# TensorE in a written order from the 24th head on, with shorter transposes, in a window attention and feed-forward kernel

## The chip, the cores and the metric

The kernel runs on one core of a Trainium2 chip. Its engines are TensorE (PE: matmuls; PEld: the loads of the stationary operand), VectorE (DVE), ScalarE (ACT), GpSimd (POOL) and SyncE (SP, which issues most DMAs here). The metric is the device time of one execution, in microseconds; lower is better. Three runs of the kernel before were timed.

## The reference

Two layers follow each other. Attention over 8 batches and 8 heads (512 local and 32 global positions, head size 64), in which a local query sees the 32 global keys and local keys at a distance of at most 32, and a global query sees everything; then a feed-forward layer over all 4352 rows.

```python
# attention, per batch and head; D = 64, window = 32, scale = 1/8
k_all, v_all = concat(k_g, k_l), concat(v_g, v_l)
out_g = softmax(scale * q_g @ k_all.T) @ v_all
s_ll = where(abs(i - j) <= 32, scale * q_l @ k_l.T, -1e9)
s_l = concat(scale * q_l @ k_g.T, s_ll)
out_l = softmax(s_l) @ v_all
x = rows of concat(out_g, out_l), heads side by side        # 4352 x 512
# feed-forward, d_model 512, d_ff 2048; s and b are scalars
r = relu(x @ w_in)
out = (s * r * r + b) @ w_out
```

## The kernel before

**Slots.** A *slot* j is one head of one half of the 512 local positions: 8 batches x 2 halves x 8 heads = 128 slots, 16 per batch. The 256 queries of a slot are two blocks of 128; each block has its keys in two chunks. `CHUNKS` gives for each chunk its first key column `c0`, the first query row `q0` that it serves and the number `n` of such rows: one chunk serves all 128 rows, the other one only 64 or 96 of them.

**Precision.** From slot `NF` = 16 on, and in the feed-forward layer throughout, operands are split into a high part (fp32r) and a low one, and products are sums of several matmuls over these parts. The first 16 slots use plain f32 matmuls (`scores32`, `transposes32`, `pv32`).

**A split slot.** `scores(j)`: four matmuls into `ps_s` (L362), and one into `ps_g` (L368) for the global queries; then `softmax(j)` on DVE, ACT and DVE (L213, L219, L226). `p_transposes(j)`: four TensorE transposes of the probabilities `sm` into `ps_t` (L310), split by ACT and DVE (L378, L379). `pv_products(j)`: four matmuls into `ps_o` (L389), summed in `pv_sum` (L400 to L403) into the tile `x`. `transposes_and_pv(j-1, j-2)` mixes the transposes of the slot before with the products of the one before that, two and two.

**Global queries.** Per batch and group g of four heads: `g_softmax` at slot 16b + G_AT[g], `g_transposes` three slots later (four chunks "early", the fifth "late" in the slot, L441; evacuated by L444 and L445), `g_load` (a DMA and splits on ACT and POOL) and `g_pv` (ten matmuls, L463) in the slots after. The results go to DRAM (`xg_d`). The transposes of heads and of global groups use one and the same PSUM buffer, tag "t".

**Feed-forward.** 17 token tiles of 256 rows (16 of the two halves of the batches, the last one of the global rows), 8 steps each: step m does `ffn_in(m)` (24 matmuls of 256 columns, L511; then ACT L517, DVE L518, ACT L525 and DVE L526 make `g`) and `ffn_out(m)` (12 matmuls of 512 columns, L543). `x_split(t)` (L483, L484) makes a tile's operand `xs`, which has a single buffer. The last tile's operand comes from `xg_split`, which loads two row blocks from `xg_d` into buffers of tag "r" (two buffers, used by the feed-forward steps too), transposes each (L494) and splits it (L496, L497).

**Weights.** w_in and w_out arrive as 64-bit integers in 32 pieces and are decoded on ACT and DVE in slots 0 to 13 (`PIECES`).

**What sets the order.** The text is a loop over j; in pass j stand the scores of slot j, the transposes of j - 1, the products of j - 2, ffn_in of m = j - LAG and ffn_out of m - 1. The framework's planner turns this into one instruction stream per engine: at each moment of its own timeline it takes, of the instructions that are ready, the one that stands first in the text. So the text gives priorities and the planner's costs the order. `tc.manual_schedule(engines=...)` fixes an engine's order to that of the text; the kernel before doesn't use it. Each engine then executes its stream strictly in that order and waits for what each instruction needs.

Of the kernel before, what the change touches and what calls it, by code (L numbers as in the profile page):

```python
# [10 lines left out]
F32 = mybir.dt.float32  # L11
# [10 lines left out]
P = 128  # L22
# [21 lines left out]

NF = 16
AHEAD = 0
LAG = 12
WARM_FIRST = 28
WARM_HEAD = 0

# [2 lines left out]
NORM_POOL = lambda j: j < NF  # L53
ACT_DMA = 2
X_ACT = lambda j: j >= 8
G_AT = (13, 18)
G_TR = 3
G_LD = (0, 2)
G_PV = (1, 3)
# [9 lines left out]
def window_attention_then_ffn(ctx: ExitStack, tc: tile.TileContext, qd, qg, kw, vw, vg, w_in, w_out, sv, bv, out):  # L69
    nc = tc.nc  # L70
# [4 lines left out]
    ps = ctx.enter_context(tc.tile_pool(name="ps", bufs=1, space=bass.MemoryType.PSUM))  # L75
# [3 lines left out]
    ident = const.tile([P, P], F32, name="ident")  # L79
# [9 lines left out]
    def keep_busy(n, name):  # L89
        p_w = ps.tile([P, 512], F32, tag="acc1", name=name)  # L90
        for _ in range(n):
            nc.tensor.matmul(p_w, lhsT=warm[:, 0:P], rhs=warm, start=True, stop=True)
# [5 lines left out]
    for first, parts in ((True, ((32, 192, 0),)), (False, ((0, 160, 0), (192, 224, 32)))):  # L98
# [3 lines left out]
        for c0, c1, skip in parts:  # L102
            for sign, base in ((1, c0 - skip), (-1, 64 - c0 + skip)):
                nc.gpsimd.affine_select(
                    out=mask[:, c0:c1], in_=mask[:, c0:c1], pattern=[[sign, c1 - c0]], compare_op=ALU.is_ge,
# [56 lines left out]
    st_ = {}  # L162

    def slot(j):
        return j // 16, (j // 8) % 2, j % 8
# [38 lines left out]
    def softmax(j, p_s):  # L204
        b, hf, h = slot(j)
        sm = sb.tile([P, NC], F32, tag="sm", name=f"sm{j}")
        nm = sb.tile([P, 2], F32, tag="nm", name=f"nm{j}")
        ss = sb.tile([P, 2], F32, tag="ss", name=f"ss{j}")
        cols = [COLS[hf, blk] for blk in range(2)]
        for blk in range(2):  # L210
            c = cols[blk]
            mask = masks[hf == 0 and blk == 0][:, 0:c.stop - c.start]
            nc.vector.tensor_tensor_reduce(  # L213
                out=sm[:, c], in0=p_s[:, c], in1=mask,
                op0=ALU.add, op1=ALU.min, scale=-scale, scalar=BIG, accum_out=nm[:, blk:blk + 1],
            )
        for blk in range(2):
            p = sm[:, cols[blk]]
            nc.scalar.activation(  # L219
                out=p, in_=p, func=AF.Exp, bias=nm[:, blk:blk + 1], scale=-1.0, accum_out=ss[:, blk:blk + 1],  # L220
            )
        nc.vector.tensor_scalar_add(ss, ss, 1e-9)
        nc.vector.reciprocal(ss, ss)
        for blk in range(2):
            p = sm[:, cols[blk]]
            (nc.gpsimd if NORM_POOL(j) else nc.vector).tensor_scalar(  # L226
                out=p, in0=p, scalar1=ss[:, blk:blk + 1], scalar2=1.0, op0=ALU.mult, op1=ALU.mult,
            )
        st_["p", j] = sm


    def own(k, hf):
        n, c = (192, P) if hf == 0 else (240, 144)
        return k[:, 0:2 * n].rearrange("p (k c) -> p k c", k=2)[:, :, 0:c]

    def sg_rows(j):
        b, hf, h = slot(j)
        if hf == 0 and h % 4 == 0:
            st_["sg", b, h // 4] = sb.tile([P, SGW], F32, tag=f"sg{h // 4}", name=f"sg{j}", bufs=1)
        r0 = 32 * (h % 4)  # L240
        return st_["sg", b, h // 4][r0:r0 + 32]
# [30 lines left out]
    def scores32(j):  # L272
        b, hf, h = slot(j)
        if WARM_HEAD and j < LAG:
            keep_busy(WARM_HEAD, f"warm{j + 1}")
# [15 lines left out]
    def chunks(j):  # L291
        b, hf, h = slot(j)
        o = 0
        for blk in range(2):
            for c in range(2):
                c0, q0, n = CHUNKS[hf, blk][c]
                yield blk, c, c0, q0, n, slice(o, o + n)
                o += n
# [4 lines left out]
    def p_transposes(j):  # L303
        sm = st_.pop(("p", j))
        p_t = ps.tile([P, 512], F32, tag="t", name=f"ps_t{j}")
        first = 64 if slot(j)[1] == 0 else 0
        st_["pst", j] = p_t[:, first:first + NC]
        for blk, c, c0, q0, n, o in chunks(j):
            at = first + o.start - q0
            nc.tensor.transpose(out=p_t[:, at:at + P], in_=sm[:, c0:c0 + P], identity=ident)  # L310
            if c == 1:
                yield

    def transposes32(j):
        list(p_transposes(j))
# [39 lines left out]
    def scores(j):  # L355
        b, hf, h = slot(j)
        ks, qs = st_.pop(("ks", j)), st_.pop(("qs", j))
        p_s = ps.tile([P, 512], F32, tag="s", name=f"ps_s{j}")
        for blk in range(2):
            cols = COLS[hf, blk]  # L360
            for a in range(2):
                nc.tensor.matmul(  # L362
                    p_s[:, cols], lhsT=qs[:, a, blk * P:(blk + 1) * P], rhs=ks[:, cols], start=(a == 0), stop=(a == 1),
                )
        p_g = ps.tile([P, 512], F32, tag="g", name=f"ps_g{j}")
        qgh = st_["qgs", b][:, h]
        ng = 256 + 32 * hf
        nc.tensor.matmul(p_g[0:64, 0:ng], lhsT=qgh, rhs=own(ks, hf), start=True, stop=True)  # L368
        softmax(j, p_s)

        tg = sb.tile([P, 288], F32, tag="tg", name=f"tg{j}", bufs=1)
        nc.scalar.copy(out=tg[0:32, 0:ng], in_=p_g[32:64, 0:ng])
        nc.vector.tensor_add(out=sg_rows(j)[:, hf * 256:hf * 256 + ng], in0=p_g[0:32, 0:ng], in1=tg[0:32, 0:ng])
# [11 lines left out]
    def pv_products(j):  # L385
        pt, vs = st_.pop(("pt", j)), st_.pop(("vs", j))
        p_o = st_["pso", j] = ps.tile([P, 2, 2, P], F32, tag="o", name=f"ps_o{j}")
        for blk, c, c0, q0, n, o in sorted(chunks(j), key=lambda x: (x[0], -x[1])):
            nc.tensor.matmul(  # L389
                p_o[:, blk, :, q0:q0 + n], lhsT=vs[:, 2 * blk + c], rhs=pt[:, :, o], start=(c == 1), stop=(c == 0),  # L390
            )
            if c == 0:
                yield

    def pv_sum(j):
        b, hf, h = slot(j)
        p_o = st_.pop(("pso", j))
        x = x_tile(j)
        u = sb.tile([P, 2, P], F32, tag="u", name=f"u{j}", bufs=1)
        nc.scalar.copy(out=u, in_=p_o[:, :, 1, :])  # L400
        nc.vector.tensor_add(out=u, in0=p_o[:, :, 0, :], in1=u)
        q0 = 64 * (h % 2)
        nc.vector.tensor_add(  # L403
            out=x[q0:q0 + 64, h // 2, :].rearrange("p (k q) -> p k q", k=2), in0=u[0:64], in1=u[64:128],
        )


    def transposes_and_pv(jt, jp):
        t = p_transposes(jt) if NF <= jt < NS else iter(())
        p = pv_products(jp) if NF <= jp < NS else iter(())  # L410
        for _ in range(2):
            next(p, None)
            next(t, None)
        list(p), list(t)
        if NF <= jp < NS:
            pv_sum(jp)
        if NF <= jt < NS:
            p_split(jt)
# [145 lines left out]
    extra, early, late = defaultdict(list), {}, {}  # L564
    for b in range(B):
        for g in range(2):
            s0 = 16 * b + G_AT[g]
            extra[s0].append(lambda b=b, g=g: g_softmax(b, g))
            early[s0 + G_TR] = lambda b=b, g=g: g_transposes(b, g, 0, 4)
            late[s0 + G_TR] = lambda b=b, g=g: g_transposes(b, g, 4, 5)  # L570
            for i in range(2):
                h = 4 * g + 2 * i
# [13 lines left out]
    sp = pick(lambda j: None, split)  # L586
    vl, vl32 = pick(lambda j: None, v_load), pick(v_load32, lambda j: None)
    sc = pick(scores32, scores)
    tr = pick(transposes32, lambda j: None)
    vsp = pick(lambda j: None, v_split)  # L590
    pvs = pick(pv32, lambda j: None)
    piece = 0
    qg_load(0)
    ld(0)
    ld(1)
    for j in range(NM + LAG + 2):
        sp(j + 1)
        ld(j + 2)
        vl(j)
        for _ in range(PIECES[j] if j < len(PIECES) else 0):  # L600
            weight_piece(piece)
            piece += 1
        if j < NS:
            b1 = j // 16 + 1
            if j == 14 and NF > 16:
                qg_load32(1)
            elif j % 16 == 14 and b1 < B:
                qg_load(b1)
            sc(j)
            if j == NF - 1 and NF % 16:  # L610
                if NF > 16:
                    qg_load(j // 16)
                qg_split(j // 16)
            if j % 16 == 15 and NF <= j + 1 < NS:
                qg_split(b1)
        if j in early:
            early.pop(j)()
        m = j - LAG
        if m == 0:
            x_split(0)  # L620
        if 0 <= m < NM:
            ffn_in(m)
            if m % 8 == 7:
                t = m // 8 + 1
                if t < 16:
                    x_split(t)
                elif t == 16:
                    xg_split(16)
        tr(j - 1)
        transposes_and_pv(j - 1, j - 2)  # L630
        vsp(j - 1)
        for fn in extra.pop(j, []):
            fn()
        pvs(j - 2)
        vl32(j)
        if 0 <= m - 1 < NM:
            ffn_out(m - 1)
        if j in late:
            late.pop(j)()
    assert piece == 32 and not extra  # L640


# [66 lines left out]
```

## Time and profile before

| | |
|---|---|
| time, median of 3 runs | 1067.21 us (1065.12 to 1070.13) |
| the profiled execution's own time | 1068.86 us |
| its span, first to last instruction | 1067.1 us |
| TensorE busy | 1039.9 us (97%) |
| VectorE / ScalarE / GpSimd busy | 813.6 / 706.9 / 330.7 us |
| mean granted TensorE clock | 0.966 |
| bytes moved | 86.79 MB |

The page also follows back the chain of work that ended last. 93% of it is on PE: ffn_in 36%, ffn_out 35%, the transposes of heads 6%, scores 4%, products 4%. The busy time of PE has modelled ends, so the spacing of its instructions is read from the chain, in which a group's time runs to the start of the next.

### The profile page before, as it was taken

How to read it: one execution, taken by the hardware profiler on the slowest of the kernel's cores; microseconds unless marked ns; L12 is line 12 of the kernel's file. 1: busy time of each engine (PE TensorE's matmuls, PEld its weight loads, DVE VectorE, ACT ScalarE, POOL GpSimd, SP SyncE). 2: the span in 40 equal slices, each digit the busy share in tenths (PEclk: the TensorE clock that was granted, in tenths of full speed). 3: DMA queues.
4: the chain of work that ended last, by engine and by line, in shares of the span. 5: the costliest groups of instructions: out<-in, count | busy, mean ns of one | idle time of the engine just before them, and what ended most of it. 6: DMA issues, size and time to landing. Idle time of an engine off the chain costs nothing.

```text
span 1067.1 us, 20496 instructions
## 1 busy us (share of the span) xinstructions
PE 1039.9 (97%) x7076; PEld 932.2 (87%) x7076; DVE 813.6 (76%) x2116; ACT 706.9 (66%) x1796; POOL 330.7 (31%) x397
## 2 busy tenths in 40 slices
PE   6989999999999999999999999999999999999996
PEld 2558899999999999999999999999999999999895
DVE  6789777997788887888788877888788878853221
ACT  5667676786677776786678766867677767743221
POOL 3222433442343342342344233434234224211000
PEclk7558999999999999999999999999999999999999
DMA  7656321321323131221122122312122122100000
GB/s 248 199 180 209 96 86 52 93 92 34 97 68 98 53 97 52 90 79 60 58 92 84 56 80 69 95 56 84 60 79 89 53 72 77 59 14 34 22 20 20
DMA packets 63535, 86.79 MB, mean 81 GB/s; under 512 B 7624, under 2 KB 50632, under 8 KB 63432
## 3 DMA queue, kind: packets, MB, share of 16 engines
q1 hardware_dynamic: 63144, 84.44, 25.1%
q8 instruction: 56, 0.92, 0.3%
q10 hardware_dynamic: 288, 1.05, 0.3%
q14 instruction: 47, 0.39, 0.1%
HBM read 76.02 MB, written 9.44 MB: 80 GB/s over the span
## 4 chain that ended last, share of the span: by engine, by line
PE 93%; DMA 2%; ACT 2%; DVE 2%; POOL 1%; issue 0%; SPq 0%; ACTq 0%; DVEq 0%; POOLq 0%
PE ps_h L511 36%; PE acc L543 35%; PE ps_t L310 6%; PE ps_s L362 4%; PE ps_o L389 4%; PE ps_og L463 2%; PE ps_o L327 2%; PE ps_s L281 1%; PE ps_g L368 1%; DMA wst<-in_w_in 1%; PE ps_g L287 1%; PE ps_tg L441 1%; DMA rk<-in_kw 1%; POOL sm L226 0%; DMA wst<-in_w_out 0%
## 5 line engine op out<-in xcount | busy, mean ns | idle before, releaser
L511 PE MATMUL ps_h<-xs,wi 128*128 128x256 f32 x3264 | 449.8, 286 | 0.9 <-ACT xs L496 0.7
L511 PEld LDWEIGHTS ps_h<-xs,wi 128*128 128x128 f32 x3264 | 418.0, 190 | 11.1 <-ACT xs L483 0.9
L543 PE MATMUL acc<-wo,g 128*128 128x512 f32 x1632 | 417.3, 395 | 0.0
L543 PEld LDWEIGHTS acc<-wo,g 128*128 128x128 f32 x1632 | 292.2, 188 | 54.0 <-ACT x L333 0.5
L518 DVE SCALAR_TENSOR_TENSOR r<-ps_h,s_t,r 128x512 f32<-128x512 f32 x136 | 101.5, 746 | 79.1 <-ACT r L517 78.9
L201 POOL TENSOR_TENSOR vs<-rv,vs 128x256 fp32r<-128x256 f32 x112 | 85.3, 761 | 190.7 <-ACT vs L200 190.3
L526 DVE SCALAR_TENSOR_TENSOR g<-r,b_t,g 128x512 fp32r<-128x512 f32 x136 | 109.3, 804 | 45.1 <-ACT g L525 41.7
L525 ACT ACTIVATE g<-r,b_t 128x512 fp32r<-128x512 f32 x136 | 98.4, 724 | 65.0 <-DVE r L518 64.8
L517 ACT ACTIVATE r<-ps_h 128x512 f32<-128x512 f32 x136 | 81.2, 597 | 87.5 <-PE ps_h L511 79.7
L193 POOL TENSOR_TENSOR kq<-rq,kq 128x256 fp32r<-128x256 f32 x112 | 89.3, 797 | 149.1 <-ACT kq L192 130.4
L219 ACT ACTIVATE sm<-sm,nm 128x224 f32<-128x224 f32 (+1 forms) x256 | 118.3, 465 | 24.4 <-DVE nm L213 23.6
L310 PE MATMUL ps_t<-ident,sm 128*128 128x128 f32 x512 | 100.6, 288 | 4.2 <-POOL sm L226 4.2
L191 POOL TENSOR_TENSOR kq<-rk,kq 64x416 fp32r<-64x416 f32 x56 | 63.1, 1127 | 121.0 <-ACT kq L190 105.4
L213 DVE CUSTOM_DVE_ANT_0 sm<-ps_s,mask 128x224 f32<-128x224 f32 (+1 forms) x256 | 85.8, 367 | 16.1 <-PE ps_t L310 9.5
L455 POOL TENSOR_TENSOR vsg<-rvg,vsg 128x320 fp32r<-128x320 f32 x64 | 58.0, 927 | 98.2 <-ACT vsg L454 98.2
L389 PE MATMUL ps_o<-pt,vs 128*128 128x256 f32 x448 | 83.7, 283 | 0.1
L403 DVE TENSOR_TENSOR x<-u 64x256 f32<-64x256 f32 x112 | 71.0, 634 | 3.6
L362 PE MATMUL ps_s<-kq 128*128 128x192 f32 (+1 forms) x448 | 72.9, 275 | 0.0
L310 PEld LDWEIGHTS ps_t<-ident,sm 128*128 128x128 f32 x512 | 58.2, 145 | 14.8 <-POOL sm L226 7.4
L362 PEld LDWEIGHTS ps_s<-kq 128*128 128x128 f32 x448 | 65.3, 190 | 5.1
L226 DVE TENSOR_SCALAR sm<-sm,ss 128x192 f32<-128x192 f32 (+1 forms) x224 | 66.9, 341 | 3.2
L389 PEld LDWEIGHTS ps_o<-pt,vs 128*128 128x128 f32 x448 | 66.8, 190 | 2.1 <-DVE pt L379 0.6
(79 smaller groups left out, 1232.4 us busy)
## 6 DMA issues: line engine op xcount, KB each, us to landing
rq<-in_qd SPq DMA_DIRECT2D x128, 128.0 KB, 2.1
rv<-in_vw SPq DMA_DIRECT2D x128, 128.0 KB, 2.0
rk<-in_kw SPq DMA_DIRECT2D x64, 208.0 KB, 2.4
rvg<-in_vg SPq DMA_DIRECT2D x32, 320.0 KB, 2.9
out<-o SPq DMA_DIRECT2D x34, 256.0 KB, 2.1
wst<-in_w_in SPq DMA_DIRECT2D x15, 512.0 KB, 4.5
wst<-in_w_out SPq DMA_DIRECT2D x15, 512.0 KB, 4.5
rqg<-in_qg SPq DMA_DIRECT2D x8, 128.0 KB, 2.0
```

The costliest lines, as they stand in the source:

```text
L193: nc.gpsimd.tensor_sub(out=qs[:, 1, :], in0=rq, in1=f32(qs[:, 0, :]))
L201: nc.gpsimd.tensor_sub(out=vs[:, :, 1, :], in0=rv4, in1=f32(vs[:, :, 0, :]))
L213: nc.vector.tensor_tensor_reduce(out=sm[:, c], in0=p_s[:, c], in1=mask, op0=ALU.add, op1=ALU.min, scale=-scale, scalar=BIG, accum_out=nm[: ...
L219: nc.scalar.activation(out=p, in_=p, func=AF.Exp, bias=nm[:, blk:blk + 1], scale=-1.0, accum_out=ss[:, blk:blk + 1],)
L310: nc.tensor.transpose(out=p_t[:, at:at + P], in_=sm[:, c0:c0 + P], identity=ident)
L362: nc.tensor.matmul(p_s[:, cols], lhsT=qs[:, a, blk * P:(blk + 1) * P], rhs=ks[:, cols], start=(a == 0), stop=(a == 1),)
L389: nc.tensor.matmul(p_o[:, blk, :, q0:q0 + n], lhsT=vs[:, 2 * blk + c], rhs=pt[:, :, o], start=(c == 1), stop=(c == 0),)
L511: nc.tensor.matmul(p_h[:, k], lhsT=wi[:, a, c, f * P:(f + 1) * P], rhs=xs[:, e, c, :], start=(n == 0), stop=(n == 11),)
L518: nc.vector.scalar_tensor_tensor(out=r, in0=p_h, scalar=s_t, in1=r, op0=ALU.mult, op1=ALU.mult)
L525: nc.scalar.activation(out=g[:, 0], in_=r, func=AF.Identity, bias=b_t)
L526: nc.vector.scalar_tensor_tensor(out=g[:, 1], in0=r, scalar=b_t, in1=f32(g[:, 0]), op0=ALU.add, op1=ALU.subtract,)
L543: nc.tensor.matmul(oacc[t][i], lhsT=g[:, a, k, i * P:(i + 1) * P], rhs=wo[:, e, f, :], start=(pr == 0 and n == 0), stop=(pr == 7 and n == 5),)
```

## The change

- `LAG` is 10 in place of 12: each feed-forward step stands two slots earlier in the text, and the loop has two passes less.
- From pass j = `ORDERED` = 24 on, PE's instructions are issued in the order of the text. The other engines are left to the planner.
- In a pass, transposes and products now stand ahead of ffn_in (with the v splits and v loads that follow them), and the early global transposes behind it.
- `G_AT` is (12, 16) in place of (13, 18).
- A chunk that serves 64 or 96 rows from row 0 is transposed with 96 rows in place of 128; the short chunks of both blocks come first.
- Transposes and products alternate two products, three transposes, two products, one transpose.
- The matmul into `ps_g` stands between two of the four matmuls of the scores.

```diff
-LAG = 12
+LAG = 10
+ORDERED = 24
-G_AT = (13, 18)
+G_AT = (12, 16)
 ...
         first = 64 if slot(j)[1] == 0 else 0
         st_["pst", j] = p_t[:, first:first + NC]
-        for blk, c, c0, q0, n, o in chunks(j):
+        for blk, c, c0, q0, n, o in sorted(chunks(j), key=lambda x: x[1]):
             at = first + o.start - q0
-            nc.tensor.transpose(out=p_t[:, at:at + P], in_=sm[:, c0:c0 + P], identity=ident)
-            if c == 1:
-                yield
+            q = 96 if c == 0 and q0 == 0 else P
+            nc.tensor.transpose(out=p_t[:, at:at + q], in_=sm[0:q, c0:c0 + P], identity=ident[0:q, 0:q])
+            yield
 ...
             for a in range(2):
                 nc.tensor.matmul(
                     p_s[:, cols], lhsT=qs[:, a, blk * P:(blk + 1) * P], rhs=ks[:, cols], start=(a == 0), stop=(a == 1),
                 )
-        nc.tensor.matmul(p_g[0:64, 0:ng], lhsT=qgh, rhs=own(ks, hf), start=True, stop=True)
+                if blk == hf and a == 0:
+                    nc.tensor.matmul(p_g[0:64, 0:ng], lhsT=qgh, rhs=own(ks, hf), start=True, stop=True)
 ...
                 p_o[:, blk, :, q0:q0 + n], lhsT=vs[:, 2 * blk + c], rhs=pt[:, :, o], start=(c == 1), stop=(c == 0),
             )
-            if c == 0:
-                yield
+            yield
 ...
-        for _ in range(2):
-            next(p, None)
-            next(t, None)
+        for which in (p, p, t, t, t, p, p, t):
+            next(which, None)
         list(p), list(t)
 ...
+    fixed = ExitStack()
     for j in range(NM + LAG + 2):
+        if j == ORDERED:
+            fixed.enter_context(tc.manual_schedule(engines={mybir.EngineType.PE}))
         sp(j + 1)
 ...
-        if j in early:
-            early.pop(j)()
+        tr(j - 1)
+        transposes_and_pv(j - 1, j - 2)
+        vsp(j - 1)
+        pvs(j - 2)
+        vl32(j)
         m = j - LAG
         if m == 0:
             x_split(0)
 ...
-        tr(j - 1)
-        transposes_and_pv(j - 1, j - 2)
-        vsp(j - 1)
+        if j in early:
+            early.pop(j)()
         for fn in extra.pop(j, []):
             fn()
-        pvs(j - 2)
-        vl32(j)
         if 0 <= m - 1 < NM:
             ffn_out(m - 1)
         if j in late:
             late.pop(j)()
+    fixed.close()
```

More of the change, by code (lines that the diff above doesn't have):

```diff
@@ L358, in scores @@
         p_s = ps.tile([P, 512], F32, tag="s", name=f"ps_s{j}")
+        p_g = ps.tile([P, 512], F32, tag="g", name=f"ps_g{j}")
+        qgh = st_["qgs", b][:, h]
+        ng = 256 + 32 * hf
         for blk in range(2):
@@ L364, in scores @@
                 )
[L365 to L368, printed above, removed]
+                if blk == hf and a == 0:
+                    nc.tensor.matmul(p_g[0:64, 0:ng], lhsT=qgh, rhs=own(ks, hf), start=True, stop=True)
         softmax(j, p_s)
```

## The prediction

> **What bounds the kernel now.** I read the page first, then the chain of work in order of time, the groups of instructions split by shape, the sums by stretch and, for the end, the order of time around the last token tile.
>
> ```profile
> span 1067.1 us, 20496 instructions
> PE 1039.9 (97%) x7076; PEld 932.2 (87%) x7076; DVE 813.6 (76%) x2116; ACT 706.9 (66%) x1796; POOL 330.7 (31%) x397
> 0.00:50.00 50.00, 38.24 (x121) 19.26 (x122) 35.48 (x93) 27.55 (x62) 13.02 (x24) 0.65 0.64 218
> 50.00:100.00 50.00, 45.60 (x205) 32.15 (x205) 42.98 (x113) 36.36 (x84) 13.05 (x14) 0.67 0.61 200
> 550.80:667.30 116.50, 116.50 (x837) 108.11 (x835) 96.88 (x259) 84.51 (x222) 41.83 (x49) 1.00 0.24 74
> L511 PE MATMUL ps_h<-xs,wi 128*128 128x256 f32 x329 | 51.0, 298 | 0.0
> L362 PE MATMUL ps_s<-kq 128*128 128x192 f32 (+1 forms) x32 | 5.1, 276 | 0.0
> 551.41 2.30 PE ps_h L511 x19
> 900.59 2.30 PE ps_h L511 x19
> ```
>
> TensorE is the bound. In the stretch rows (columns: stretch, length, busy time of PE, PEld, DVE, ACT, POOL, granted clock, DMA share, GB/s) it is busy for the whole of a stretch in mid-run at clock 1.00; only the first 100 us have gaps and a low clock (0.65, 0.67). The last two rows of that fence are the same place of the head loop, three batches (48 slots) apart: 349.18 us, so 116.39 us per batch of 16 slots, 7.27 us per slot. Nothing that leaves TensorE's stream alone can move this time. The two groups of 329 and 32 matmuls are the first 184.4 us: 8 split heads scored (j = 16 to 23) and 329/24 = 13.7 feed-forward steps. The planner has thus run at a distance of 10.3 already when slot 24 begins, where the written order takes over with LAG = 10. So the new LAG by itself costs and gains nothing there.
>
> **The written order, priced row by row.** The chain's rows give what each block costs from its start to the start of what follows.
>
> ```profile
> 954.51 2.88 PE ps_h L511 x24
> 981.65 2.76 PE acc L543 x12
> 767.77 0.60 PE ps_og L463 x10
> 792.45 0.13 PE ps_g L368
> 792.93 0.42 PE ps_s L362 x4
> 789.56 0.21 PE ps_o L389 x2
> 789.77 0.22 PE ps_t L310 x2
> 789.99 0.18 PE ps_o L389 x2
> 790.18 0.23 PE ps_t L310 x2
> 794.56 0.33 PE ps_t L310 x3
> 765.95 0.09 PE ps_o L389
> ```
>
> A slot in written order is ffn_in 2.88, ffn_out 2.76, scores 0.42, global scores 0.13, products and transposes 0.21 + 0.22 + 0.18 + 0.23 = 0.84: 7.03 us. Sixteen are 112.48. Per batch come two global groups, each five transposes at 0.11 (0.33/3) and two products at 0.60: 3.50. Sum 115.98 against 116.39 measured: the planner's scattering costs 0.4 per batch, and the order gives it back.
>
> *The new turn of products and transposes* (two, three, two, one) has as many changes from one kind to the other as the old: nothing. *Global scores inside the scores*: a 192-column matmul steps in 0.09 where a cheap weight load follows (last row), and in 0.42/4 = 0.105 on average in the scores. Bounds 0 and 0.015 x 16 = 0.24 per batch; I take 0.15, since both halves of a batch put it behind a 192-column one.
>
> *Transposes with 96 rows.* No such shape is in the trace. What a transpose's step consists of is read from the durations (by shape, mid-run; mean ns before the last bar):
>
> ```profile
> L389 PEld LDWEIGHTS ps_o<-pt,vs 128*128 128x128 f32 x257 | 38.5, 190 | 0.8
> L310 PEld LDWEIGHTS ps_t<-ident,sm 128*128 128x128 f32 x258 | 28.2, 140 | 0.4
> L463 PEld LDWEIGHTS ps_og<-vsg,pg 128*64 128x64 f32 x160 | 11.5, 135 | 0.0
> L310 PE MATMUL ps_t<-ident,sm 128*128 128x128 f32 x259 | 48.4, 276 | 0.0
> L463 PE MATMUL ps_og<-vsg,pg 128*64 128x128 f32 x160 | 12.2, 222 | 0.0
> ```
>
> The transpose's weight load (140 ns) is as short as one of 64 columns (135), not like one of 128 (190), while its matmul (276) is longer than another one over 128 columns (222). So its 0.11 us step is the moving side, which the edit cuts by a quarter: 0.027 us where another transpose follows, nothing where a wide weight load does. The sort puts the short chunks first, so they are followed by transposes. One per head in the first half of a batch, two in the second: 24 per batch, 0.65 us. Bounds 0 and 0.65; I take 0.65 by the two load rows. [...]
>
> Per batch 0.41 + 0.15 + 0.65 = 1.2 us; slots 24 to 127 are 6.5 batches: **-7.8 us**. Before slot 24 only the shorter transposes count, some 20 of them at full clock: **-0.5**.
>
> **What the fixed order adds.** First, the one-chunk global transpose stands at the end of its slot and the next head's transposes are now early in the next slot; both use the single buffer "t". The edge, where the planner had something else to run:
>
> ```profile
> 870.95 0.27 PE L441 MATMUL ps_tg<-ident,sg 128*128 128x128 f32 x1
> 871.26 0.27 ACT L444 CAST pg<-ps_tg 128x128 fp32r<-128x128 f32 x1 [2.61 <-PE ps_tg L441]
> 871.60 0.27 DVE L445 TENSOR_TENSOR pg<-ps_tg,pg 128x128 fp32r<-128x128 f32 x1
> ```
>
> The buffer is free 871.87 - 870.95 = 0.92 us after that transpose starts. In the new order 0.11 + 0.42 + 0.13 + 0.20 = 0.86 us of work lie between. At best the wait is 0.06 plus the transpose's own weight load behind it; with VectorE in the middle of another instruction (0.75 us ones run then) up to 0.7. I take 0.25, near the good end, 13 times: **+3.2** (0.8 to 9).
>
> Second, the last token tile. xg_split's transposes come right after ffn_in(127) in the text and now stay there.
>
> ```profile
> 1001.79 3.04 PE L511 MATMUL ps_h<-xs,wi 128*128 128x256 f32 x24
> 1004.67 2.93 PE L543 MATMUL acc<-wo,g 128*128 128x512 f32 x12
> 1007.44 0.60 PE L494 MATMUL ps_xg<-ident,xgr 128*128 128x128 f32 x4
> 1010.68 0.63 PE L494 MATMUL ps_xg<-ident,xgr 128*128 128x128 f32 x4
> 1012.71 7.86 PE L511 MATMUL ps_h<-xs,wi 128*128 128x256 f32 x64 [0.22 <-DVE xs L497]
> L491 SPq DMA_DIRECT2D xgr<-xg_d x2: 338/340/341, 1002.2 to 1008.1; - x2
> DMA to landing us min/median/max: 2.4/2.4/2.5
> ```
>
> The second load was issued at 1008.1, when the first four transposes had ended (1007.44 + 0.60) and so freed their buffer; it landed 2.4 us later. From the first transposes to the second: 3.24 us, in which the planner ran ffn_out(127). Now nothing may run there: 0.44 of transposes and 2.8 us idle. Then ffn_out(126) covers the copies. From the end of ffn_in(127) to ffn_in(128): 3.24 + 0.44 + 2.76 = 6.4 with one ffn_out still owed, 9.2 in all, against 7.8 now (1004.67 to 1012.71, less the two matmuls of L511 that ran earlier): **+1.4**.
>
> The other moves are hidden. The head products, v_split and the global transposes change places in the text, with their POOL splits and the rvg loads on SP's queue one or two slots earlier; POOL has 41.83 of 116.50 us busy, DMA a share of 0.24, each of these results has a slot (7.27 us) before its use, and what would be late next is ffn_out's g (rival below). Up to slot 9 the text of the program is unchanged, so the gaps of the first 100 us should stay; the planner fills them from later text, though, and I allow 4 us either way, 0 in the sum.
>
> Sum: -7.8 - 0.5 + 3.2 + 1.4 = -3.7 us. The profiled execution took 1068.9 by the clock of the runs (span 1067.1), 1.7 above the median of 1067.2; set against the median the forecast is **1063.5 us**, -0.35%; its own range, with late-transpose waits from 0.1 to 0.45 each and 2 us of the start, 1060 to 1067. A measurement here can't tell less than about 0.5% (5.3 us) from no change.
>
> **Rivals.**
> *A, no waits at all*: the late transpose's wait vanishes behind the weight load, the gain stays whole: 1067.2 - 8.3 + 1.4 = 1060.3, with 2 us from the start 1058. For it: PE waits for nothing for hundreds of us now. Against: the 0.92 against 0.86.
>
> *B, VectorE becomes what TensorE waits for* (the other side).
>
> ```profile
> L518 DVE SCALAR_TENSOR_TENSOR r<-ps_h,s_t,r 128x512 f32<-128x512 f32 x136 | 101.5, 746 | 79.1 <-ACT r L517 78.9
> L526 DVE SCALAR_TENSOR_TENSOR g<-r,b_t,g 128x512 fp32r<-128x512 f32 x136 | 109.3, 804 | 45.1 <-ACT g L525 41.7
> L484 DVE TENSOR_TENSOR xs<-x,xs 128x512 fp32r<-128x512 f32 x32 | 21.1, 683 | 0.2
> ```
>
> It has 96.88 of 116.50 us to do, 83%. At a tile boundary ffn_in(8t+8) must follow x_split, which can start only when ffn_in(8t+7) has ended; between them lie 2.76 + 0.42 + 0.13 + 0.84 = 4.15 us, in which VectorE has 0.75 + 0.80 + 2 x 0.68 = 2.9 of this alone, on top of softmax and pv sums. The planner could slide other matmuls in; a written order can't. At 0.26 us in each of 14 boundaries the gain is gone; at 0.65 the kernel is slower by 0.5%; at 0.85, 1063.5 + 11.9 = 1075.
>
> *C, the 96 rows save nothing* (weight load bound after all): 1063.5 + 0.65 x 6.5 + 0.5 = 1068.2.
>
> *D, the tail gap is long.* If the second load of xg_split gets the buffer of r instead, it waits for g's end, 1007.85 - 1004.67 = 3.2 us after ffn_in(127), and lands at 5.6: +2.5 us and a gap of 5.2. The clock then matters:
>
> ```profile
> 1057.00:1058.00 1.00, 0.71 (x4) 0.24 (x2) 0.00 (x0) 0.74 (x2) 0.00 (x0) 1.00 0.00 0
> 1062.00:1063.00 1.00, 0.00 (x0) 0.00 (x0) 0.00 (x0) 0.00 (x0) 0.00 (x0) 0.92 0.26 102
> ```
>
> After the last matmul (1057.71) the granted clock fell within 1062 to 1063, some 5.1 us later. Falling to half for about 4 us would add 2: 1068. The gap of 2.8 in my sum is well short of that. [...]
>
> **How the numbers follow.** Forecast 0.37, A 0.28, B 0.17, C 0.09, D 0.09. Under 1061.9 (faster): most of A (0.22), 0.15 of the forecast, 0.02 of the others with a lucky start: 0.39. Over 1072.5 (slower): B beyond 0.65 us, 0.13, and 0.02 of the rest: 0.15. Same: 0.46. The range 1057 to 1073 leaves out A with a good start (0.06) and B's far part (0.12).
>
> **What would show it.** Right: the batch pattern recurs in some 115.2 us; the 96-row matmul lasts about 27 ns less than 276; PE waits at the transposes for L445's successor, some 0.25 us, 13 times; one idle stretch of 2.8 us before the second xg transposes. Wrong: waits of ffn_in at tile boundaries on VectorE's xs, a clock below 1.00 near the end, transposes stepping 0.11 as before, or a first 100 us that is more than 4 us shorter or longer.

## The result, and the profile after

The changed kernel takes 1083.91 us (median of 4 runs, 1079.78 to 1085.6), the kernel before 1066.16 (1065.08 to 1070.13): a ratio of 1.0143, 95% interval 1.0122 to 1.0163. It is slower by 17.75 us; the forecast was 1063.5 with a range up to 1073. Executions in a slower state are left out of all times below (one of e11's kernel, 1250.49 us at a mean clock of 0.742, and one of the kernel before, 2216.19 us).

The profiled execution is the quickest of the four, 1079.78 us. The head of its page (the span and the busy time of each engine), its waits of TensorE (instruction <- what it waited for: us in total, times, longest) and its first two stretches:

```profile
span 1077.9 us, 20536 instructions
PE 1036.5 (96%) x7076; PEld 928.2 (86%) x7076; DVE 817.3 (76%) x2116; ACT 708.6 (66%) x1796; POOL 324.4 (30%) x397
```

```profile
PE ps_tg L441 <- DVE pt L381: 12.9, 12, 1.2
...
PE ps_g L370 <- DVE sg L375: 2.5, 1, 2.5
...
```

```profile
0.00:50.00 50.00, 42.15 (x129) 21.03 (x129) 38.20 (x101) 31.09 (x69) 12.37 (x26) 0.64 0.72 242
50.00:100.00 50.00, 44.24 (x221) 33.12 (x221) 44.06 (x112) 34.20 (x80) 11.09 (x13) 0.75 0.56 187
```

TensorE's work has hardly changed (1036.5 us busy against 1039.9), and the number of matmuls is the same. Its idle time has grown from 27.2 us (1067.1 - 1039.9) to 41.4 (1077.9 - 1036.5): the 10.8 us that the span has grown are waits that were not there. The first line of the waits is the main one. The two stretches say why this execution is quicker than its three fellows, as far as can be said: its start was a good one, with more bytes per second (242 against 218 GB/s in the first 50 us) and a higher granted clock in the second 50 (0.75 against 0.67 before). The other three have no trace, only their mean clock (0.961 to 0.964 against 0.966).

**The early global transposes.** The order of time around one of them in the kernel before (L310 and L379 are L312 and L381 of the changed kernel), then around one of the 12 waits; columns: start, duration, engine, line, operation, tiles, and in brackets what the engine had waited for. The last row is the same place five batches later.

```profile
273.56 0.38 PE L310 MATMUL ps_t<-ident,sm 128*128 128x128 f32 x2
...
275.73 0.58 DVE L379 TENSOR_TENSOR pt<-ps_t,pt 128x416 fp32r<-128x416 f32 x1
...
279.56 0.60 PE L441 MATMUL ps_tg<-ident,sg 128*128 128x128 f32 x4
```

```profile
269.69 0.27 PE L312 MATMUL ps_t<-ident,sm 128*128 128x128 f32 x1
269.72 3.10 PE L511 MATMUL ps_h<-xs,wi 128*128 128x256 f32 x24
...
272.01 0.73 POOL L202 TENSOR_TENSOR vs<-rv,vs 128x256 fp32r<-128x256 f32 x1 [0.26 <-ACT vs L201]
272.12 0.91 DVE L404 TENSOR_TENSOR x<-u 64x256 f32<-64x256 f32 x1
272.31 0.49 ACT L380 CAST pt<-ps_t 128x416 fp32r<-128x416 f32 x1
273.43 0.57 DVE L381 TENSOR_TENSOR pt<-ps_t,pt 128x416 fp32r<-128x416 f32 x1
274.05 0.66 PE L441 MATMUL ps_tg<-ident,sg 128*128 128x128 f32 x4 [1.24 <-DVE pt L381]
...
863.61 0.66 PE L441 MATMUL ps_tg<-ident,sg 128*128 128x128 f32 x4 [1.23 <-DVE pt L381]
```

The last transpose of a head (L312) ends at 269.96. Behind it stand the 24 matmuls of ffn_in, 2.9 us, and then the global transposes (L441), which write the same buffer "t". That buffer is free when ACT (L380) and VectorE (L381) have split the head's probabilities: L381 ends at 274.00, 4.0 us after the last transpose. TensorE waits 1.24 us, and its stream lets nothing else pass: the ffn_out behind it (L543) starts at 274.46, though its g was written by 268.98 (L526). Before, the planner ran other matmuls there: L441 starts 5.6 us after the last transpose (279.56 - 273.94), and the split had ended at 276.31. The wait stands twice in a batch; a batch takes (863.61 - 274.05)/5 = 117.91 us. The two waits cost 2.58 of it by the spacing of the matmuls (1.14 and 1.44), which leaves 115.33, against 116.39 before.

**The late ones and the shorter transposes.** First the late transpose and the next head's first three, in order of time. Then transposes by shape in mid-run, mean ns before the last bar. Then, from the chain of the changed kernel, two groups of three transposes, with one short one among them and with two.

```profile
277.30 0.27 PE L441 MATMUL ps_tg<-ident,sg 128*128 128x128 f32 x1
...
278.26 0.52 PE L312 MATMUL ps_t<-ident,sm 128*128 128x128 f32 x3
```

```profile
L312 PE MATMUL ps_t<-ident,sm 128*128 128x128 f32 x158 | 41.9, 281 | 0.0
...
L312 PE MATMUL ps_t<-ident,sm 96*128 96x96 f32 x94 | 18.4, 249 | 0.0
...
L312 PEld LDWEIGHTS ps_t<-ident,sm 96*128 96x128 f32 x94 | 11.2, 142 | 0.4
```

```profile
307.66 0.33 PE ps_t L312 x3
...
314.62 0.29 PE ps_t L312 x3
```

From the late transpose to the next head's are 0.96 us, with 0.86 of work between: a wait of 0.1 (over all of them, 0.19 by the spacing). A short transpose lasts 32 ns less, and in the chain's rounded steps three of them with two short ones take 0.29 us; that is 0.02 less for each short one than 0.11 x 3. Its weight load is as long as that of a long one before (142 against 140).

**The end.** Order of time around the last token tile, then three stretches of half a microsecond with the granted clock (third column from the right):

```profile
1008.37 3.04 PE L511 MATMUL ps_h<-xs,wi 128*128 128x256 f32 x24
...
1011.60 0.66 PE L494 MATMUL ps_xg<-ident,xgr 128*128 128x128 f32 x4 [0.20 <-DMA xgr<-xg_d]
...
1013.55 0.56 ACT L496 CAST xs<-ps_xg 128x512 fp32r<-128x512 f32 x1
...
1014.34 0.68 DVE L497 TENSOR_TENSOR xs<-ps_xg,xs 128x512 fp32r<-128x512 f32 x1
1015.08 1.11 PE L494 MATMUL ps_xg<-ident,xgr 128*128 128x128 f32 x4 [2.82 <-DVE xs L497]
...
1015.85 5.32 PE L543 MATMUL acc<-wo,g 128*128 128x512 f32 x12
```

```profile
1013.50:1014.00 0.50, 0.00 (x0) 0.00 (x0) 0.33 (x1) 0.50 (x2) 0.00 (x0) 1.00 0.64 205
1014.00:1014.50 0.50, 0.00 (x0) 0.00 (x0) 0.50 (x2) 0.11 (x1) 0.00 (x0) 0.54 0.64 246
...
1020.50:1021.00 0.50, 0.50 (x2) 0.37 (x2) 0.00 (x0) 0.00 (x0) 0.00 (x0) 0.63 0.00 0
```

TensorE is idle for 2.82 us, as long as foreseen. Two things end together there. The one that the prediction named, the second load, was issued at 1012.3, when the first transposes had ended, and landed 2.6 us later (L491), at about 1014.9. The last one is the evacuation of the first transposes (L496, L497, to 1015.02), which ACT and VectorE come to only after their share of ffn_in(127), and which the prediction did not count. And the clock falls in that gap, at 1014.0, and is back only at 1020.9. The ffn_out in between takes 5.32 us instead of the 2.93 before.

### The profile page after: what moved, and what is told of

Same layout as the page of the kernel before. It is cut to its first block, busy times and chain, and to the rows that moved or that the text cites. A ratio compares the mean times of both kernels' runs of the same rounds, so it can differ in the third digit from the quotient of the medians.

```text
span 1077.9 us, 20536 instructions
## 1 busy us (share of the span) xinstructions
PE 1036.5 (96%) x7076; PEld 928.2 (86%) x7076; DVE 817.3 (76%) x2116; ACT 708.6 (66%) x1796; POOL 324.4 (30%) x397
## 4 chain that ended last, share of the span: by engine, by line
PE 80%; DVE 11%; ACT 4%; issue 2%; DMA 2%; SPq 0%; DVEq 0%; ACTq 0%
PE acc L543 32%; PE ps_h L511 30%; PE ps_t L312 4%; PE ps_s L366 4%; PE ps_o L391 3%; PE ps_og L463 1%; DVE x L404 1%; PE ps_o L328 1%; PE ps_s L282 1%; PE ps_g L370 1%; DVE g L526 1%; DVE pt L381 1%; PE ps_tg L441 1%; DMA wst<-in_w_in 1%; DVE u L402 1%
## 5 line engine op out<-in xcount | busy, mean ns | idle before, releaser
L511 PE MATMUL ps_h<-xs,wi 128*128 128x256 f32 x3264 | 428.5, 286 | 0.0
L511 PEld LDWEIGHTS ps_h<-xs,wi 128*128 128x128 f32 x3264 | 404.3, 190 | 5.8 <-ACT pt L319 0.9
L543 PE MATMUL acc<-wo,g 128*128 128x512 f32 x1632 | 404.2, 395 | 0.0
L543 PEld LDWEIGHTS acc<-wo,g 128*128 128x128 f32 x1632 | 297.6, 189 | 56.2 <-DVE g L526 0.3
L526 DVE SCALAR_TENSOR_TENSOR g<-r,b_t,g 128x512 fp32r<-128x512 f32 x136 | 118.0, 868 | 56.3 <-ACT g L525 55.8
L518 DVE SCALAR_TENSOR_TENSOR r<-ps_h,s_t,r 128x512 f32<-128x512 f32 x136 | 101.1, 743 | 67.1 <-ACT r L517 66.9
L202 POOL TENSOR_TENSOR vs<-rv,vs 128x256 fp32r<-128x256 f32 x112 | 89.4, 798 | 56.6 <-ACT vs L201 51.3
L312 PE MATMUL ps_t<-ident,sm 128*128 128x128 f32 (+1 forms) x512 | 99.5, 279 | 1.7 <-POOL sm L227 1.3
L391 PE MATMUL ps_o<-pt,vs 128*128 128x256 f32 x448 | 90.0, 284 | 0.0
L374 ACT COPY tg<-ps_g 32x256 f32<-32x256 f32 (+1 forms) x112 | 42.2, 377 | 68.1 <-PE ps_g L370 67.2
L366 PEld LDWEIGHTS ps_s<-kq 128*128 128x128 f32 x448 | 71.6, 189 | 7.3
L402 DVE TENSOR_TENSOR u<-ps_o,u 128x256 f32<-128x256 f32 x112 | 47.1, 421 | 35.7 <-ACT u L401 33.8
L312 PEld LDWEIGHTS ps_t<-ident,sm 128*128 128x128 f32 (+1 forms) x512 | 59.1, 146 | 11.5 <-issue 6.1
L391 PEld LDWEIGHTS ps_o<-pt,vs 128*128 128x128 f32 x448 | 67.5, 190 | 0.3
```

The lines of the kernel that those rows point to most:

```text
L202: nc.gpsimd.tensor_sub(out=vs[:, :, 1, :], in0=rv4, in1=f32(vs[:, :, 0, :]))
L312: nc.tensor.transpose(out=p_t[:, at:at + q], in_=sm[0:q, c0:c0 + P], identity=ident[0:q, 0:q])
L366: nc.tensor.matmul(p_s[:, cols], lhsT=qs[:, a, blk * P:(blk + 1) * P], rhs=ks[:, cols], start=(a == 0), stop=(a == 1),)
L391: nc.tensor.matmul(p_o[:, blk, :, q0:q0 + n], lhsT=vs[:, 2 * blk + c], rhs=pt[:, :, o], start=(c == 1), stop=(c == 0),)
L511: nc.tensor.matmul(p_h[:, k], lhsT=wi[:, a, c, f * P:(f + 1) * P], rhs=xs[:, e, c, :], start=(n == 0), stop=(n == 11),)
L518: nc.vector.scalar_tensor_tensor(out=r, in0=p_h, scalar=s_t, in1=r, op0=ALU.mult, op1=ALU.mult)
```

## The experiments

The theory from this trace: the loss is the shared buffer "t" at the early global transposes. Rivals: the 96-row transposes (rows of another shape, another mask), the end, the new LAG, or the written order as such. Ratios are to the kernel before, timed beside it on the same chip.

**The early transposes into another buffer** (e1)

```diff
-            p_t = ps.tile([P, 4, P], F32, tag="t", ...)
+            p_t = ps.tile([P, 4, P], F32, tag="s" if c0 == 0 else "t", ...)
```

> The changed kernel, with the early global transposes put into the PSUM buffer of the scores (tag s, free by then) in place of the buffer t that they share with the heads' transposes. Theory 'one buffer': in the changed kernel's profile TensorE waits 12 times 1.1 to 1.4 us (15.5 us in all by the spacing of its instructions) until VectorE has taken the head's transposes out of t; with another buffer these waits vanish, so about 15 us less than the changed kernel, 1067 to 1069, and the batch pattern goes from 117.9 to about 115.5 us. Rival 'VectorE is the bound': it only comes late everywhere, and the wait returns at the next thing that needs it (ffn_out's g, x_split, the products): under 5 us gained.

1064.24 us (1058.86 to 1069.36, 10 runs), ratio 0.9973 (0.9951 to 0.9995): 19.7 us less than the changed kernel, by one tag (18 by the two ratios), and more than the 15 expected. The line L441 <- L381 is gone from the waits, and so is the one of slot 24 (L370 <- L375), where the written order takes over (2.7 us by the spacing, which the expectation had not counted); the one at the end stays:

```profile
PE ps_xg L494 <- DVE xs L497: 3.0, 1, 3.0
```

```profile
990.00:1000.00 10.00, 7.93 (x54) 6.99 (x53) 2.69 (x4) 3.11 (x5) 0.00 (x0) 1.00 0.17 52
1000.00:1010.00 10.00, 9.03 (x54) 8.03 (x55) 2.44 (x5) 2.40 (x5) 0.00 (x0) 1.00 0.01 3
```

The first transposes are at 997.3, so the wait lies in these two stretches, and the clock stays at 1.00: the same gap, 0.2 us longer, lowered it in one execution and not in the other. It lowered it in the traces of e3 and e6 too (gaps of 3.0 and 2.8 us, half clock from 1019.9 and 1013.9 on), so in three of four.

**The end given back to the planner** (e2)

```diff
+        if j == NM + LAG - 9:          # ffn_in(127)
+            fixed.close()
         sp(j + 1)
 ...
-    fixed.close()
```

> The changed kernel, with the written order ended at the pass of ffn_in(127), so that the planner is free again for the last token tile. Theory 'tail gap and clock': the transposes of the last tile left TensorE idle for 3 us and at half clock for 6.5 us; both go, 4.6 us by the profile's spacing, more if the slower runs of the changed kernel (up to 1085.6 against 1079.8 of the profiled one, at a lower mean clock) owe that to a longer time at half clock there: 1075 to 1079, and the runs lie closer together. Rival 'the clock falls somewhere else': 4 to 5 us less and the same scatter.

1080.57 us (1080.15 to 1081.32), ratio 1.013 (1.0114 to 1.0146): 3.3 us less than the changed kernel by the medians, with intervals of the two ratios that overlap, and short of the 1075 to 1079 expected. The total alone doesn't show the gain; the traces do. From the start of ffn_in(127) to the end of the program are 65.5 us (1078.0 - 1012.51) against 69.5 in the changed kernel (1077.9 - 1008.37) and 65.3 before. The clock stays whole through the last tile:

```profile
1010.00:1020.00 10.00, 10.00 (x59) 8.70 (x58) 3.60 (x5) 3.24 (x5) 0.00 (x0) 1.00 0.13 30
1020.00:1030.00 10.00, 9.02 (x66) 8.00 (x65) 2.29 (x4) 2.56 (x5) 0.00 (x0) 1.00 0.14 51
```

**All transposes with 128 rows** (e3)

```diff
-            q = 96 if c == 0 and q0 == 0 else P
+            q = P
```

> The changed kernel, with every chunk transposed with 128 rows; order and everything else as changed. If the transpose's step is its moving side, as predicted: 0.65 us per batch more, 4.5 to 5 us slower than the changed kernel, 1088 to 1089, and the shorter transposes' 0.08 us steps become 0.11. Rival 'weight load bound': no difference.

1082.1 us (1077.88 to 1083.21), ratio 1.0136 (1.0111 to 1.0162). The expectation missed: no difference to the changed kernel (1083.91). The row says where the longer transposes went:

```profile
PE ps_tg L441 <- DVE pt L381: 8.3, 12, 0.7
```

12 waits as before, but 8.3 us together instead of 12.9. The edit changed more than TensorE's rows: the planner, which still orders the other engines, here puts ACT's L380 ahead of L201, so GpSimd's L202 comes later. The place that the changed kernel has at 272.01 to 274.00:

```profile
276.51 0.42 DVE L404 TENSOR_TENSOR x<-u 64x256 f32<-64x256 f32 x1
...
277.04 0.57 DVE L381 TENSOR_TENSOR pt<-ps_t,pt 128x416 fp32r<-128x416 f32 x1
277.05 0.73 POOL L202 TENSOR_TENSOR vs<-rv,vs 128x256 fp32r<-128x256 f32 x1 [1.13 <-ACT vs L201]
```

L404 no longer runs beside L202 and takes 0.42 us instead of 0.91. L381 ends 3.45 us after the last transpose (277.61 - 274.16) instead of 4.04, and the wait is 0.66 instead of 1.24. So the waits shrank because the split ended sooner, about as much as the longer transposes cost, and this run can't price the 96 rows.

**e1 and e2 together** (e4; both edits above)

> Both repairs together: early global transposes in the scores' buffer, and the written order ended at the last token tile. If the two losses are independent, the gains add: 15 + 5 to 9 us under the changed kernel, 1060 to 1064, which is faster than the kernel before. Rival 'VectorE is the bound': 1070 or more.

1062.59 us (1056.85 to 1065.27, 9 runs), ratio 0.9956 (0.9938 to 0.9974): faster than both kernels (than the kernel before by 0.4%), as expected, and the two gains add up to about what they were alone (21.3 us against 19.7 + 3.3). A batch takes 115.66 us by the recurrence of the early transposes.

**Everything but the written order** (e5)

```diff
-ORDERED = 24
+ORDERED = 10000
```

> The changed kernel without the written order: ORDERED beyond the last pass, all other edits kept, so that the planner orders TensorE throughout. Theory 'the order's waits are what was lost': the early waits (15.5 us), the handover at slot 24 (2.7) and the tail (4.6 or more) all go, and of the gain the 96-row transposes stay (4 to 5 us) while the tidier order (0.4 per batch) is lost: 1060 to 1065. Rival 'the reordered text or the shorter LAG cost the time': 1075 or more.

1075.7 us (1071.63 to 1077.39), ratio 1.009 (1.0064 to 1.0115). The expectation missed: without the written order the text is still 0.9% slower than before. The waits of TensorE, and one of them in order of time:

```profile
PE ps_h L511 <- DVE xs L484: 9.9, 7, 1.5
```

```profile
266.60 1.02 DVE L484 TENSOR_TENSOR xs<-x,xs 128x512 fp32r<-128x512 f32 x1
...
267.68 2.51 PE L511 MATMUL ps_h<-xs,wi 128*128 128x256 f32 x19 [1.55 <-DVE xs L484]
```

That is x_split of the next tile, late at seven of the tile boundaries. With LAG = 10, x_split(t) stands in the pass of the last sum into its tile x, one pass ahead of the ffn_in that needs it. The rival of the expectation came true; the next run tells its two halves apart.

**The planner with the old LAG** (e9: e5 with one more edit)

```diff
-LAG = 10
+LAG = 12
```

> The changed kernel without the written order and with LAG = 12 as before; the other edits kept (turn of products and transposes, 96 rows, global scores inside, G_AT, places in the text). Without the written order and with LAG = 10 the profile shows ffn_in waiting 1.5 us for x_split's VectorE part at every second tile boundary or more (2 to 3.5 us per batch by the spacing), and 1075.7 us. Theory 'the shorter LAG leaves x_split no time when the planner orders TensorE': with LAG 12 these waits go, 13 to 15 us less, 1060 to 1064. Rival 'the new places in the text do it': still 1070 or more.

1064.66 us (1059.02 to 1067.66, 10 runs), ratio 0.9971 (0.9956 to 0.9986). The waits for xs are gone, and with them 11 us (1075.7 - 1064.66; 13 to 15 were expected): under the planner the shorter LAG costs that. What is left of the change then (96 rows, the new turns, the new places in the text) is worth 0.3%.

**The split of the probabilities first** (e6; the changed kernel with p_split at a higher priority)

```diff
-            p_split(jt)
+            with tc.high_priority():
+                p_split(jt)
```

> The changed kernel with the buffers as they are, but with the split of the heads' transposes (ACT copy and VectorE subtraction) at high priority for the planner. In the changed kernel these two stand behind seven ACT and four VectorE instructions and end 4.0 us after the transposes, 1.4 us after ffn_in. Theory 'one buffer, and its evacuation comes late in two queues': the split ends within 2 us, the early waits go as with another buffer: 12 to 17 us less than the changed kernel, 1067 to 1072. Rival 'VectorE is full': what was overtaken comes late in its place, under 5 us gained.

1079.31 us (1078.01 to 1082.55), ratio 1.0134 (1.011 to 1.0157). The expectation missed. The edit barely did what it was meant to (lines behind it count one more, so L442 is L441 here):

```profile
272.80 0.27 PE L312 MATMUL ps_t<-ident,sm 128*128 128x128 f32 x1
...
276.18 0.59 DVE L381 TENSOR_TENSOR pt<-ps_t,pt 128x416 fp32r<-128x416 f32 x1
...
276.83 0.66 PE L442 MATMUL ps_tg<-ident,sg 128*128 128x128 f32 x4 [0.91 <-DVE pt L381]
```

The split ends 3.7 us after the transposes (276.77 - 273.07) instead of 4.0, and the wait is 0.91 instead of 1.24. It moved in the sense of the theory, but by too little to decide anything; the 4.6 us gained are what the rival allowed.

**The fifth global chunk with the other four** (e7: e4, and no late transpose any more)

```diff
-            p_t = ps.tile([P, 4, P], F32, tag="s" if c0 == 0 else "t", ...)
+            p_t = ps.tile([P, 4, P], F32, tag="s" if c0 == 0 else "g", ...)
 ...
-            early[s0 + G_TR] = lambda b=b, g=g: g_transposes(b, g, 0, 4)
-            late[s0 + G_TR] = lambda b=b, g=g: g_transposes(b, g, 4, 5)
+            early[s0 + G_TR] = lambda b=b, g=g: (g_transposes(b, g, 0, 4), g_transposes(b, g, 4, 5))
```

> Both repairs, and the fifth chunk of the global groups transposed together with the four others, into the buffer of the global scores (tag g), in place of the end of the slot. In the kernel with both repairs 12 waits of 0.3 us are left where that late transpose holds buffer t or s: they go, 3.5 to 4 us, so 1058 to 1060, 0.7% under the kernel before. Rival 'the wait moves to tag g (the global scores or products)': 1062 to 1063 as with both repairs.

1062.29 us (1059.41 to 1064.21, 12 runs), ratio 0.9962 (0.9947 to 0.9976): no gain that can be measured over e4; the expectation (1058 to 1060) missed, and its rival was right. Of the 0.6 us of late waits per batch in e4 (two of 0.3) some 0.2 is won: 115.43 against 115.66. The rest returns as 0.36 at the next scores, which now wait for buffer "s".

**The same with 128 rows** (e8: e7 with the edit of e3)

> The kernel of the run before this one, with every chunk transposed with 128 rows. Where TensorE waits for nothing, the shorter transposes must show their price: by the moving side 24 x 0.027 = 0.65 us per batch, 4.5 to 5 us more than with 96 rows. In the changed kernel itself 128 rows made no measurable difference, because the early waits ran out by as much. Rival 'the weight load sets the step': no difference here either.

1065.72 us (1063.19 to 1068.49, 12 runs), ratio 0.9999 (0.9984 to 1.0013). Where the early waits are gone, the 96 rows are worth 3.4 us, somewhat less than the 4.5 to 5 expected. The same place of the loop five batches apart, first in e7, then in e8:

```profile
246.06 0.71 PE L441 MATMUL ps_tg<-ident,sg 128*128 128x128 f32 x5
...
823.21 0.71 PE L441 MATMUL ps_tg<-ident,sg 128*128 128x128 f32 x5
```

```profile
247.87 0.71 PE L441 MATMUL ps_tg<-ident,sg 128*128 128x128 f32 x5
...
826.70 0.71 PE L441 MATMUL ps_tg<-ident,sg 128*128 128x128 f32 x5
```

577.15/5 = 115.43 and 578.83/5 = 115.77: 0.34 us per batch between them, or 2.2 us over 6.5 batches. The remaining 1.2 us of the 3.4 lie within the scatter of the medians. In e8, too, the planner orders ACT otherwise (L404's median is 0.42 us against 0.52 in e7), so the totals compare more than the rows. The transposes themselves do not: in the chain, three of them with two short ones take 0.28 us in e7 and the same three 0.33 in e8, in each of six slots in a row (438.90 to 473.66, 441.08 to 476.05), 0.025 for each short one.

**The four chunks in buffer "o"** (e11: e7 with another tag)

```diff
-            ... tag="s" if c0 == 0 else "g", ...
+            ... tag="o" if c0 == 0 else "g", ...
```

> Both repairs, with the five global transposes together behind ffn_in, four in the products' buffer (tag o) and the fifth in the global scores' (tag g). With the buffer of the scores 0.36 us per batch was left at the next slot's scores; the products come 0.6 us later in a slot. If that wait goes too, 115.05 us per batch and 1059 to 1061; if VectorE's share (83%) only moves it, 1062 as before.

1063.24 us (1058.16 to 1066.49), ratio 0.9961 (0.9944 to 0.9979), the same as e7, and so the second of the two outcomes expected. The wait moves to the matmul of the global scores, for the fifth chunk's evacuation:

```profile
PE ps_g L370 <- DVE pg L445: 1.3, 6, 0.3
```

**The written order with the old LAG** (e12: e7 with LAG = 12)

> Both repairs and the five global transposes together (scores' and global scores' buffers), with LAG = 12 in place of 10. Left to the planner, the shorter LAG cost 11 us (1075.7 against 1064.7), all of it at x_split. Theory 'the written order takes that loss away': in it 4.1 us of other matmuls stand between the two ffn_in at a tile boundary, whatever the LAG, and no wait of ffn_in for xs was seen; so LAG 12 changes nothing, 1061 to 1064, and two passes more at the end cost nothing. Rival 'the shorter LAG costs something there too': 1058 or less with LAG 12.

1119.82 us (1118.58 to 1126.47), ratio 1.0497 (1.0467 to 1.0527): 57 us more than e7. Neither theory had expected that. The waits of TensorE, and the order of time around one:

```profile
PE ps_o L391 <- DVE ss L223: 21.0, 6, 3.5
PE ps_o L391 <- DVE u L402: 14.7, 7, 2.8
```

```profile
338.32 1.29 DVE L484 TENSOR_TENSOR xs<-x,xs 128x512 fp32r<-128x512 f32 x2
...
340.62 1.28 DVE L404 TENSOR_TENSOR x<-u 64x256 f32<-64x256 f32 x1
...
342.47 0.40 DVE L402 TENSOR_TENSOR u<-ps_o,u 128x256 f32<-128x256 f32 x1
343.01 0.71 PE L391 MATMUL ps_o<-pt,vs 128*128 128x256 f32 x2 [3.49 <-DVE ss L223]
```

The tile x has one buffer. With LAG = 12, x_split(t) follows ffn_in(8t - 1), the last to read the old xs, in pass 8t + 11, whereas the first sum into the next x (slot 8t + 8) already stands in pass 8t + 10. That sum (L404) must wait until x_split (L484) has read the old x; u and ps_o are held meanwhile (ACT's L401, which refills u, waits for L404), and the products (L391) stand at the head of TensorE's stream. With LAG = 10 the split falls between the last sum of one tile and the first of the next, and there is no such wait. The planner could take ffn_in first; the written order can't. The two rows of waits are 35.7 of the 57 us. The clock is a further part: between 200 and 1000 us it stood at 0.50 eight times for 3.4 us (342.8 to 346.2 here), up to 14 us by an estimate from that. The rest was not added up.

## Why the prediction was wrong

**What failed** is the step "The other moves are hidden ... each of these results has a slot (7.27 us) before its use". It asked when the *inputs* of the moved early transposes are there, and they are. It didn't ask when their *output buffer* is free. The buffer "t" is filled in the same slot, by the transposes that the change put ahead of ffn_in, and its evacuation ends 4.0 us later with only 2.9 us of ffn_in between. The prediction priced just this for the late transpose, some paragraphs earlier, and for the early ones, 12 of them, it took 0. They cost (1.14 + 1.44) x 6 = 15.5 us, and e1, which takes them away by a tag and the takeover's 2.7 us with them, is 19.7 us faster. e3 and e6 fit: at the place shown, the wait is as much shorter as the split ends sooner after the transposes (0.58 for 0.59 us in e3, 0.33 for 0.34 in e6).

**What wasn't thought of** is the takeover. In slot 24 the stream of the planner ends and the written one begins, and the planner had put off the global scores of the slot before; the next ones come so close behind them that they wait 2.5 us for their buffer (L370 for L375, above), some 2.7 us by the spacing. Its size is an accident of where the planner stands: with other tags it was not to be seen in e1, 0.7 in e7 and 3.8 in e11, where after two waits, of 0.62 and 1.34 us, the clock also stood at 0.50 from 191.3 to 194.7.

**The size of the end.** "+1.4" became about +4.6 (by the spacing of the matmuls: 6.1 us beyond the work in the changed kernel against 1.5 before). The gap was right (2.8 us), and the clock was not: "well short of that" rested on one row at the end of the program, 5.1 us, and here the clock fell 2.8 us after ffn_in's last matmul (about 1011.25) and 1.8 us after the end of the transposes (1012.26). e1 tells the two apart: with the same gap and a whole clock, ffn_in(127) to the end takes 66.9 us (1061.2 - 994.26), 1.6 more than before, so the gap was priced well; the changed kernel's 69.5 are 2.6 more than that, with the clock. e2, where the planner fills the gap and the clock is whole, is back at 65.5. Rival D had the falling clock, but hung it on a longer gap. What brings the fall about the runs don't show. It is not the length of the gap alone: e1's 3.0 us left the clock whole and 2.8 us here did not. Nor was TensorE always idle for long before it: in e11 the clock fell at 191.3, with a matmul at 189.87, and in e5 at 620.6, behind a wait of 1.55 us for xs that ended at 620.46.

**What came as priced.** The batch without its new waits takes 115.33 us with both late waits in it, or 115.43 in e7 and 115.66 in e4; the forecast was 115.2 + 2 x 0.25 = 115.7. The late transposes wait 0.19 us (0.25 predicted). The 96 rows are worth 0.02 to 0.03 us per transpose in the chain (0.027 predicted) and 3.4 us in all (e8 against e7, predicted 0.65 x 6.5 + 0.5 = 4.7; by the batch alone 2.2), so rival C, that they save nothing, falls: the step follows the moving side (the matmul lasts 249 ns against 281, the weight load 142 against 140). One sentence of the prediction is not so: "Up to slot 9 the text of the program is unchanged". The first 16 slots use the same `p_transposes`, so the shorter transposes and their new order stand in the text from the first slot on; the 4 us either way cover that. Rival A, no wait at all, is what e7 comes nearest to, at 1062.29.

**Rival B** had the right sign and the right kind (VectorE's work is what TensorE waits for, in an order that can't slide), but the wrong place: in the changed kernel no wait of ffn_in for x_split shows. It does show in e5, under the planner, which runs ffn_in early and finds xs late.

**"The new LAG by itself costs and gains nothing."** In the changed kernel no wait shows that comes of the shorter LAG. It is not a property of the number, though: under the planner LAG = 10 costs 11 us (e5 against e9), and in the written order LAG = 12 costs 57 (e12 against e7).

**The account.** Predicted: stream -7.8, start -0.5, late waits +3.2, end +1.4; sum -3.7. Measured: stream with late waits 6.5 x (115.33 - 116.39) = -6.9, early waits +15.5, takeover +2.7, end 6.1 - 1.5 = +4.6; with the -0.5 taken over, +15.4. The medians differ by 17.75; the 2.3 us between are no more than one execution of this kernel and another differ by (1079.78 to 1085.6). The start alone differs by that: e2's kernel has the same stream on TensorE up to the last token tile, and its trace comes to the takeover's wait (L370, 2.46 us in both) at 193.04, 4.0 us later than the changed kernel's at 189.04.

**What stays open.** The three unprofiled runs of the changed kernel were 3 to 6 us longer than the profiled one. A start like e2's (215 GB/s, clock 0.71 in the second 50 us) would make 1083.8 us of the profiled 1079.78 and so account for it; that it was so is not shown. Nor do the times settle whether the written order itself gains anything: with both waits mended it stands at 0.9962 (e7), and the planner with LAG = 12 and nearly the same text at 0.9971 (e9), with intervals that overlap. By the traces a batch takes 115.43 us in e7 and 115.7 in e9 (L441 at 268.16 and, five batches later, at 846.55), so in mid-run the order is worth about 0.25 us per batch, under 2 us in all.

## What to carry to other kernels

When an instruction is moved in a written order, price two times for it: when its inputs are there, and when its output buffer is free, counted from the last writer *in the new order* through the evacuation on the other engines; another tag may be all it takes. In a fixed stream a distance such as LAG must fit the number of buffers at both ends of the hand-over (x and xs here), and the good value under a planner may be a bad one there. And an edit on one engine can change the order that a planner gives the others (e3): before a saving is priced by a run, compare the neighbours' order, and mend the waits that they end.

## What the runs showed of the hardware

An instruction of VectorE took twice its time beside one of GpSimd. All of the changed kernel's L404 instructions (shortest, median, longest, in ns):

```profile
L404 DVE TENSOR_TENSOR x<-u x112: 420/507/994, 149.5 to 961.9; 64x256 f32<-64x256 f32 x112
```

The one at 272.12 above took 0.91 us, while GpSimd's L202 ran from 272.01 to 272.74; that is 0.49 more than the shortest, right ahead of L381 in the chain that ends the wait. Of the 112, the 30 that overlapped no GpSimd instruction took 0.42 us each, and all 16 of over 0.6 us ran beside one. In e3, where L202 came after it at this place, L404 took 0.42. The overlap in the changed kernel was 0.62 us and the loss 0.49; why VectorE loses time there these rows don't show.

And half a clock is kept for long: from 1014.0 to 1020.9 us, though dense matmuls ran again from 1015.85. One idle gap of 2.8 us thus cost about as much again in slow work as it had lasted (2.4 us in the 12 matmuls of ffn_out alone, 5.32 against 2.93). Shorter waits did it too: behind 1.55 us in e5 and behind 0.62 and 1.34 in e11 the clock fell to 0.50, both times for 3.4 us (620.6 to 624.0, 191.3 to 194.7). Other waits of that kind left it alone, five of e5's seven and the 1.2 us ones of the changed kernel; what decides it these runs don't show.
